# A two-stage spectral and feed-forward kernel: first group closed on chip by selection matmuls, weights and a third of the next input read early, other reads held

## The chip, the cores and the metric

The kernel runs on one core of a Trainium2 chip. The metric is the device time of one execution in microseconds. The profile of a run covers one execution, and its span is some 1.9 us shorter than the device time of the same run.

Some words. PE is TensorE, the engine of the matmuls; PSUM is the memory that it writes to, and an eviction is the copy of a result out of it. A clock of 1.00 is TensorE's full clock. The DMA share is the mean busy share of the 16 DMA engines, with each packet counted whole where it starts, so that it can pass 1.

## The reference

For each of 8 batches of 3136 tokens by 256 channels: a global filter in the frequency domain along the tokens, then a low-rank mixing along the tokens and a feed-forward along the channels.

```python
X = np.fft.rfft(x, axis=1)
Y = X * (filt_r + 1j * filt_i)[None, :, :]
y = np.fft.irfft(Y, n=3136, axis=1)          # per batch: 3136 x 256
...
h = y.transpose(0, 2, 1) @ U @ V             # rank 32 along the tokens
u = y + h.transpose(0, 2, 1)
out = u + np.maximum(u @ w_ch1, 0.0) @ w_ch2 # 256 -> 1024 -> 256
```

## The kernel before

The transform of length 3136 is split as 64 x 49. Stage 1 (64-point) writes its result to memory (ct1), stage 2 (49-point) reads it back in another order (tile a), its product with the filter goes through stage 3 to memory again (ct2), and stage 4 reads that (tile e) and makes the transposed input `ut` of a feed-forward group of 512 tokens. So every batch but the first makes two trips through memory before its first group. Batch 0 turns its stage 1 result on the chip and makes one.

The main loop is written by hand in steps. A group has 8 steps; each makes one 128-row tile of the first layer (two matmuls, ended by one ReLU on ScalarE) and a part of the second layer of the group before. All other work is hung onto steps:

```python
for n, gr in enumerate(groups):
    for t in range(8):
        for f, a in early[8 * n + t]: f(*a)     # products with the filter
        mm1(gr, t)                              # first layer, one tile, ReLU on ScalarE
        if n + 1 < len(groups) and t in ((2, 6) if n != 5 else (6, 7)):
            stage4(groups[n + 1], ...)          # input of the next group
        if n: mm2_part(groups[n - 1], t)        # second layer of the last group
        for f, a in plan[8 * n + t]: f(*a)      # stages 1 to 3 and reads of later batches
```

PE takes its instructions in this order and none can pass another. If the data of one small matmul are not there, the whole feed-forward stops. What is hung where, in before (cut):

```python
if b == 2: plan_st1(b, 12, (0, 1, 3, 4, 5, 7))               # stage 1 of batch 2 from step 12
elif b > 2: plan_st1(b, later(start[b - 1], -60))
m = later(start[b - 1], (5, -9, -12)[min(b, 3) - 1])         # stage 2 of batch b
...
# in stage 1 of batch b: the reads of x of batch b + 1
if 1 < b < NB - 1 and c: load_x(b + 1, c - 1)
```

Batch 1 starts at step 48 and batch 2 at step 104. I date step n by the start of its ReLU in the trace.

## Time and profile before

| | before |
|---|---|
| device time | 552.9 to 557.4 us, median 555.2 of 3 |
| first ReLU (step 0) | 62.6 us |
| step 8 (second layer joins) | 72.5 us |
| step 48 (batch 1) | 135.8 us |
| step 104 (batch 2) | 201.1 us |
| end of the span | 555.2 us |

The prediction shows the lines of the first 135 us. Here are, from the same view of windows, the two stretches after it: batch 1, then batches 2 to 7. Columns as there.

```profile
135.00:200.40 65.40, 63.91 (x567) 46.92 (x566) 43.07 (x48) 49.23 (x94) 36.11 (x22) 1.00 0.70 179
200.40:555.20 354.80, 347.32 (x3118) 259.43 (x3116) 222.91 (x256) 249.81 (x457) 159.13 (x89) 1.00 0.56 157
```

In the stretch of batch 1 PE lacks 1.5 us of being always busy.

### The profile page before, as it was taken

What the parts mean: (1) busy time and instruction counts of PE and PEld (TensorE: products, weight loads), DVE (VectorE), ACT (ScalarE), POOL (GpSimd) and SP (SyncE); (2) the same over time, 40 slices, a digit from 0 to 9 for tenths busy, and PEclk for the clock granted to TensorE, in tenths of its full rate; (3) what the DMA queues carried; (4) which work ended last, traced back from release to release, by engine and by line L of the source; (5) the groups of instructions that cost most, each with busy time, mean ns of one, the idle gap of its engine ahead of it and who ended that gap; (6) DMA issues with size and microseconds to landing.
All of it is one profiled execution on the core that took longest, in us unless ns stands there. A gap on an engine that the chain in (4) does not pass through costs nothing.

```text
span 555.2 us, 11638 instructions
## 1 busy us (share of the span) xinstructions
PE 517.2 (93%) x4491; PEld 375.3 (68%) x4491; DVE 353.1 (64%) x409; ACT 390.8 (70%) x684; POOL 282.4 (51%) x194
## 2 busy tenths in 40 slices
PE   5976689997999999999999999999999999999996
PEld 2634356664767777777776777777786777777775
DVE  6764675755756686758846785858746887643332
ACT  8566868774777688767776788677777577765663
POOL 5778179951883165915683175806563297300000
PEclk9999899997999999999999999999999999999999
DMA  9998876894669468774879468865653553333212
GB/s 194 157 170 192 225 141 187 209 230 130 174 184 250 125 176 199 173 204 137 193 222 221 123 173 228 166 199 152 186 170 121 141 167 121 106 113 115 96 77 87
DMA packets 85432, 92.06 MB, mean 166 GB/s; under 512 B 6741, under 2 KB 69416, under 8 KB 85376
## 3 DMA queue, kind: packets, MB, share of 16 engines
q1 hardware_dynamic: 67968, 75.12, 45.5%
q0 software_dynamic: 16960, 15.91, 19.1%
q8 instruction: 35, 0.57, 0.4%
q10 hardware_dynamic: 448, 0.28, 0.3%
q14 instruction: 21, 0.17, 0.1%
HBM read 57.42 MB, written 49.77 MB: 193 GB/s over the span
## 4 chain that ended last, share of the span: by engine, by line
PE 70%; POOL 10%; DVE 7%; DMA 6%; ACT 4%; issue 2%; DVEq 0%; ACTq 0%; POOLq 0%; SPq 0%
PE psum L521 25%; PE psum L488 24%; PE psum L352 4%; PE psum L344 4%; PE psum L477 4%; PE psum L497 3%; PE psum L266 3%; POOL y L634 3%; DMA x<-in_x_dram 3%; POOL x L170 2%; DVE ut L482 1%; DVE tb L632 1%; PE psum L416 1%; DMA w1sb<-in_moe_w_ch_dram 1%; ACT asb L273 1%
## 5 line engine op out<-in xcount | busy, mean ns | idle before, releaser
L492 ACT ACTIVATE hring<-psum 128x512 f16<-128x512 f32 (+1 forms) x416 | 237.7, 576 | 104.5 <-PE psum L488 103.2
L488 PE MATMUL psum<-ut,w1sb 128*128 128x512 f16 (+1 forms) x832 | 240.3, 370 | 6.4 <-ACT hring L492 3.0
L521 PE MATMUL psum<-w2sb,hring 128*128 128x256 f16 x1536 | 230.9, 273 | 0.0
L634 POOL TENSOR_TENSOR y<-ta,tb 128x1024 f16<-128x1024 f16 x56 | 120.5, 2159 | 159.4 <-DVE tb L632 115.5
L521 PEld LDWEIGHTS <-hring 128*128 128x128 f16 x1536 | 143.3, 98 | 63.8 <-issue 3.8
L482 DVE CAST ut<-psum 128x512 f16<-128x512 f32 x96 | 71.1, 741 | 108.3 <-PE psum L477 88.2
L488 PEld LDWEIGHTS <-w1sb 128*128 128x128 f16 x832 | 104.6, 145 | 27.3 <-issue 10.4
L529 DVE COPY och<-psum 128x512 f32<-128x512 f32 x96 | 66.2, 689 | 47.3 <-PE psum L497 46.6
L326 ACT CAST esb<-psum 98x512 f16<-98x512 f32 x128 | 74.7, 586 | 21.6 <-PE psum L344 16.0
L628 DVE TENSOR_TENSOR ta<-psum,fb 128x1024 f16<-128x1024 f32 x41 | 50.0, 1218 | 7.9 <-PE psum L352 6.9
L273 ACT CAST asb<-psum 128x512 f16<-128x512 f32 x78 | 45.7, 589 | 12.3 <-PE psum L266 11.2
L497 PE MATMUL psum<-idn,ut 128*128 128x128 f16 x392 | 54.0, 220 | 0.0
L477 PEld LDWEIGHTS <-e 96*128 96x128 f16 x768 | 35.9, 99 | 25.5 <-issue 10.2
L630 DVE TENSOR_TENSOR tb<-psum,fc 64x1024 f16<-64x1024 f32 x41 | 50.3, 1226 | 0.9
L632 DVE TENSOR_TENSOR tb<-psum,fc 64x1024 f16<-64x1024 f32 x41 | 49.9, 1218 | 0.8
L477 PE MATMUL psum<-sv,e 96*128 96x64 f16 x768 | 38.8, 194 | 6.5 <-DMA e<-ct 3.7
L344 PE MATMUL psum<-y,g 128*98 128x512 f16 x105 | 39.9, 380 | 3.0 <-POOL y L634 1.5
L497 PEld LDWEIGHTS <-ut 128*128 128x128 f16 x392 | 38.4, 98 | 4.9
L628 POOL TENSOR_TENSOR ta<-pc,fb 128x1024 f16<-128x1024 f16 x15 | 32.4, 2159 | 10.7 <-ACT pc L638 10.7
L352 PE MATMUL psum<-a,w2t 98*128 98x512 f16 x113 | 34.3, 379 | 1.7 <-DVE tb L632 1.6
L266 PE MATMUL psum<-x,wf 128*128 128x256 f16 x168 | 31.3, 274 | 2.8 <-DVE asb L271 1.0
L630 POOL TENSOR_TENSOR tb<-pc,fc 64x1024 f16<-64x1024 f16 x15 | 31.8, 2122 | 1.2
(93 smaller groups left out, 373.6 us busy)
## 6 DMA issues: line engine op xcount, KB each, us to landing
out_dram<-och SPq DMA_DIRECT2D x47, 512.0 KB
ct<-esb SPq DMA_DIRECT2D x64, 196.0 KB
x<-in_x_dram POOLq DMA_DIRECT2D x48, 256.0 KB, 8.1
e<-ct SPq DMA_DIRECT2D x48, 256.0 KB
a<-ct SPq DMA_DIRECT2D x56, 196.0 KB
ct<-asb SPq DMA_DIRECT2D x42, 256.0 KB
wf<-wf SPq DMA_DIRECT2D x3, 256.0 KB
w1sb<-in_moe_w_ch_dram POOLq DMA_DIRECT2D x1, 512.0 KB, 6.8
```

Of the source, the lines that this page charges most:

```text
L326: nc.scalar.copy(esb[b, k][:, 2 * half:2 * half + 2, :].rearrange("p s d -> p (s d)"), pe[0:98])
L344: nc.tensor.matmul(pe[0:98], g3[:, m, :], v, start=(n == 0), stop=(n == len(parts) - 1))
L477: nc.tensor.matmul(pu[:, 64 * i:64 * i + 64], e2[b, c][:, i, 128 * dh:128 * dh + 128], sv[:, 64 * r:64 * r + 64], start=(i == 0), stop=Tru ...
L482: nc.vector.tensor_copy(o, v)
L488: nc.tensor.matmul(ph[:, 0:n], w1sb[:, dh, :, t], gr.ut[:, dh, 0:n], start=(dh == 0), stop=(dh == 1))
L492: nc.scalar.activation(h[:, 0:n], ph[:, 0:n], RELU)
L497: nc.tensor.matmul(o[:, dh * 128:dh * 128 + 128], gr.ut[:, dh, t0:t0 + n], idn, start=False, stop=(dh == 1), skip_group_check=True)
L521: nc.tensor.matmul(o, gr.h[tt][:, i * 128:(i + 1) * 128], w2sb[:, tt, :], start=(tt == 0), stop=False, skip_group_check=True)
L529: nc.vector.tensor_copy(gr.och[:, 2 * y:2 * y + 2, :].rearrange("p j d -> p (j d)"), gr.pc)
L628: eng.tensor_mul(ta, p, va)
L630: eng.tensor_mul(tb[0:64], p[64:128], vb[64:128])
L634: nc.gpsimd.tensor_add(ys[k], ta, tb)
```

## The change

The intent is to start the feed-forward earlier. The core of the diff, with cuts marked:

```diff
+        def pick(j):                      # rows 48 to 63 of the first tile, from results on chip
+            for i in range(2):
+                sl = 2 * (j - 12) + i
+                for g in range(4):
+                    nc.tensor.matmul(zp[32 * g:32 * g + 32], sel[:, g, 28 - 4 * sl:60 - 4 * sl],
+                                     esb[0, j // 2][:, 2 * (j % 2) + i, :], start=(sl == 0), ...)
...
+                if k == 5:
+                    load_e2(0, 0, 48)     # only 48 of 64 rows go through memory
...
+    nc.gpsimd.dma_start(w2sb, moe_w_ch2...)   # second weight right behind the first
+        load_x(1, 0)                          # a third of x of batch 1 during stage 2 of batch 0
...
+    load_x(1, 1, e2[0, 0][0:1, 0, 0:1])       # the rest held until the first e tile is there
+    load_x(1, 3)
+    load_x(1, 2)
...
+    for n in (0, 3, 3, 4, 5, 5, 6, 7, 8, 9):
+        at(n, step1, 1)                       # most of stage 1 of batch 1 inside the groups
+    at(13, lambda: load_x(2, 0, a2q[0][0:1, 0:1]))
...
+    at(50, lambda: load_x(3, 0, groups[6].h[0][0:1, 0:1]))   # x of batch 3 held for batch 1's first ReLU
+    for c in range(1, 4):
+        at((50, 52, 54)[c - 1], load_x, 3, c)
...
-            plan_st1(b, 12, (0, 1, 3, 4, 5, 7))
+            plan_st1(b, 18, (0, 3, 4, 5, 7))
-            plan_st1(b, later(start[b - 1], -60))
+            plan_st1(b, later(start[b - 1], -46 if b == 3 else -60), ...)   # batch 3: from step 52
-        m = later(start[b - 1], (5, -9, -12)[min(b, 3) - 1])
+        m = later(start[b - 1], (16, -2, -12)[min(b, 3) - 1])
...
-            if n + 1 < len(groups) and t in ((2, 6) if n != 5 else (6, 7)):
+            turns = {0: (5, 6), 5: (6, 7), 12: (6, 7)}.get(n, (2, 6))
```

Cut are: the compact stage 1 table, widened on chip; the filter copies in quarters, some on GpSimd; the products on 113 partitions; the doubled form of stages 2 and 3 for four of the eight parts of batch 1.

## The prediction

> **What bounds the kernel now.** I read the windows first, cut at the landmarks of the program: the first product of batch 0's stage 2 (25.1 us), the last stage 3 of batch 0 (48.7), the first matmul of the feed-forward groups (61.2), the first product of the second layer (72.0), the first group of batch 1 (134.9), the end. Columns: stretch, its us, busy us (instructions) of each engine, TensorE clock, DMA share.
>
> ```profile
> core 0: us, PE busy (x) PEld busy (x) DVE busy (x) ACT busy (x) POOL busy (x), PEclk, DMA share, GB/s
> 0.00:25.10 25.10, 17.93 (x136) 11.68 (x137) 16.78 (x26) 16.81 (x12) 15.82 (x30) 1.00 1.02 179
> 25.10:48.70 23.60, 18.60 (x102) 9.88 (x102) 14.29 (x13) 15.90 (x24) 18.39 (x21) 0.93 1.04 178
> 48.70:61.20 12.50, 8.41 (x80) 4.99 (x80) 5.69 (x8) 8.44 (x12) 5.69 (x1) 0.86 0.81 217
> 61.20:72.00 10.80, 5.70 (x42) 3.15 (x39) 9.75 (x18) 7.78 (x10) 4.97 (x8) 1.00 0.88 198
> 72.00:134.90 62.90, 55.21 (x462) 39.30 (x462) 40.47 (x45) 42.72 (x77) 42.32 (x25) 0.95 0.75 177
> 134.90:555.20 420.30, 411.33 (x3683) 306.35 (x3681) 266.08 (x303) 299.12 (x550) 195.23 (x111) 1.00 0.58 160
> ```
>
> The last row is the bound: from 134.9 us PE is busy 411 of 420 us at full clock, and some 4 us of the rest is the tail. Nothing the change does can shorten that part. All that can be won lies before 134.9: 61.2 us until the first feed-forward matmul, 10.8 us in a group without a second layer, 62.9 us for the other five groups of batch 0.
>
> The timeline tells what paces the first part.
>
> ```profile
> 28.94 0.73 POOL L226 DMA_DIRECT2D w1sb<-in_moe_w_ch_dram  x1
> 36.00 0.57 POOL L384 DMA_DIRECT2D w2sb<-in_moe_w_ch_dram  x1 [2.07 <-DMA w1sb<-in_moe_w_ch_dram]
> 36.59 4.21 POOL L397 TENSOR_TENSOR uv<-pc,fb 128x1024 f16<-128x1024 f16 x2
> 38.77 0.59 PE L344 MATMUL psum<-uv,g 128*98 128x512 f16 x2 [2.46 <-POOL uv L397]
> 41.00 1.06 PE L344 MATMUL psum<-uv,g 128*98 128x512 f16 x2
> ...
> 52.45 1.10 SPq L438 DMA_DIRECT2D e<-ct  x2
> 57.03 2.72 PE L234 MATMUL psum<-wf 128*128 128x512 f16 x6 [0.45 <-ACT al L285]
> 61.22 0.41 PE L488 MATMUL psum<-ut,w1sb 128*128 128x512 f16 x1
> ```
>
> GpSimd could not issue the load of the second weight until the first had landed (35.7), so its product of stage 2 came late, PE idled 2.46 us, and the pair of matmuls that takes 0.59 us then took 1.06. After the last stage 3 the result goes to memory and back (e is asked for at 52.45), while PE does stage 1 of batch 1 and dummy matmuls, until 61.2. The DMA share of about 1 says that a shorter instruction chain alone would not bring this forward: the loads must shrink or be reordered.
>
> The chain of waits shows the end of batch 0.
>
> ```profile
> 102.76 2.12 POOL tb L630
> 104.94 2.13 POOL tb L632
> 107.14 1.95 POOL y L634
> 109.21 1.52 POOL x L170 x3
> 111.10 0.64 POOL x L170
> 111.74 0.54 POOL xl L163
> 112.28 2.16 POOL y L634
> 119.76 6.48 DMA ct<-esb
> 126.38 3.58 DMA e<-ct
> ```
>
> GpSimd's products and the issuing of x of batch 3 (109.2 to 112.3) delay stage 3 of batch 1. Its last store takes 6.5 us beside those 1.6 MB, and the first group of batch 1 waits 3.7 us for its data.
>
> **What the skill says.** "TensorE: Matmul & The Clock Gate", section on the HAM clock gate: PE falls to half rate after an idle window of about 3.4 us and needs one busy window to recover. The trace agrees in kind: 0.93 and 0.86 around the pause at 36.3, though that was only 2.46 us. "VectorE: DVE Perf Modes", "Why PSUM operands drop a tier": a product reading f32 PSUM runs at one element per cycle. The trace agrees: 1.22 us for 1024 elements, so fewer partitions (113 for 128) save nothing. "DMA: Bandwidth & Descriptors", "Anatomy of one DMA": about 2 us fixed per transfer, mostly the receipt. The e read's 3.58 us for 256 KB at a busy time fits, so a memory round trip cannot be below some 5 us; the change takes it off the path.
>
> **The change part by part.**
>
> *Loads.* The queue table gives 19.1% of 555 us for 15.91 MB on the GpSimd queue (6.7 us per MB of f16 landed, the f32 source being twice that) and 45.5% for 75.12 MB on the SP queue (3.4 us per MB). Check on before: wf 2.8, small constants 0.9, sv and kr 1.4, U 1.3, x 10.5, filters 10.5, V 1.3, w1 3.5, two stores 1.3: 33.5, plus a 2 us start, 35.5; w1 landed at 35.7. After: wf compact (0.41 MB) 1.4, U as f32 1.35, constants with the selection tables 1.5, x 10.5, filters 10.5, V 1.3, w1 3.5, one store 0.7: w1 at 32.5. Then w2 3.5 and the last filter row 0.5: 37. Then a third of x of batch 1, 3.5: 41.5. The other two thirds (7 us of engine time) are held until the first tile of batch 0 has come back.
>
> *Stage 2 of batch 0.* Only two transposed tiles, not four, precede the first product, and x lands 2 us sooner; VectorE must first finish a quarter of the U work (3 instructions, 1.5 us). First product at about 22.7, for 25.1. VectorE now takes 15 of 16 products (15 x 1.22) and one copy (0.7): 19 us, so the last ends at 41.9, for 47.4 by GpSimd. The last filter row (37) is in time for it. GpSimd's one product waits for its 7 us copy of V, started once w1 has landed: 39.6 + 2.1, just in time.
>
> *Closing of group 0.* Rows 48 to 63 of the first tile come from the four result tiles on chip: 64 small selection matmuls (the 32 of the low rank took 1.06 us: about 2 us), one 0.37 us copy, two 512-column matmuls. Only 48 rows pass through memory, from stores finished earlier: store 6 at about 39.5, landed 43, read back by 45.5. Then 16 matmuls 0.8, tables 0.43, a stage 1 step 0.2, low rank 0.43, eviction 0.75. First feed-forward matmul at about 48.5, for 61.2: gain 12.7.
>
> *Group 0.* Before, PE waited for 8 filter copies of 0.7 us on VectorE and four of 1.9 on ScalarE. They now lie in quarters on GpSimd and in later gaps. But ten stage 1 steps of batch 1 move in here (2 PE matmuls of 0.11 and one 0.6 or 0.7 copy each), and x must arrive: 45.5 + issue 1 + 3.5 + other traffic, 51 to 52 for the second third and 56 for the last. Eight evictions of 0.6 would be 5 us; I take 9.5, with 3 us of waits. Gain 1.3 of 10.8.
>
> *Groups 1 to 5.* PE work by counts: 40 steps x (0.43 + 0.44 + 0.055) 37; stage 4, 5 x 0.8, 4; stage 1 of batches 1 and 2, 3.3; low rank 1.1; stages 2 and 3 of batch 1, of which four of eight parts now use the doubled form (four matmuls of 0.216 more in each part, 0.86), 10.4 in all, 3.5 more than before. Sum 55.8 us. Waits I add: 2 us where stage 2 first needs batch 1 (its last stage 1 store stands on the GpSimd queue behind eight filter copies), 1 to 2 us at the first group of batch 1. x of batch 3 is held past that group, and the last parts use no GpSimd product, so the store there should take 3 us, not 6.5. 59.5 us, for 62.9: gain 3.4.
>
> *After.* The schedule starts stage 2 of batch 2 seven steps later, and five stage 1 steps of batch 3 move behind the landmark: 2 us lost.
>
> Sum: 12.7 + 1.3 + 3.4 - 2 = 15.4; 555.2 - 15.4 = 539.8, rounded to 539 for the clock (0.86 and 0.95 in two stretches cost some 4 us, of which I expect back a little).
>
> **The rivals.** (1) The wait moves to x of batch 1. Withholding two thirds until 45.5 makes stage 1 late; PE takes its instructions in order, so group 0 would stall at its fourth and seventh step. For it: the DMA share near 1 up to 72. Against: the steps are spread for these arrivals. It would cost 3 to 6 us more, 543 to 546. (2) The start is DMA-bound and gains little: if selection tables, stores and reads queue behind the weights, group 0 starts at 53. For it: the byte sum leaves only some 2 us of slack at 45. 544. (3) GpSimd becomes the bound in groups 1 to 5: filter copies at the rate of its V copy (6.95 us for 3136 elements) would take 2.2 us each, 18 us in all, delaying the last store of stage 1 and thus stage 2. Three to five us, 543. (4) All waits close: the 55.8 us stand, group 0 takes 7.5, start at 47.5: 532.
>
> **Range and chances.** The 2% line is 544.1. The start is surest (two thirds of its gain follow from removed work), the waits least. Rivals 1 to 3 together pass the line, one alone hardly. I say 539, range 531 to 548; faster 0.75, same 0.22, slower 0.03.
>
> **What would show it.** First product of stage 2 at 22 to 23.5 us, VectorE without gaps to 42; first feed-forward matmul at 47.5 to 50 with the clock near 1; w2 landed before 39; group 0 in 8 to 11 us with waits on x; first group of batch 1 at 116 to 121; from there 420 to 423 us. Wrong would be: a start after 53, a wait of over 4 us on x or on a (rivals 1, 3), or a last part longer by over 4 us, which would mean that lateness was passed on to batches 2 and 3.

## The result, and the profile after

The changed kernel took 560.9 to 562.8 us, median 561.6 of 4 runs, against a median of 555.6 of 4 for before. The ratio is 1.011, 95% interval 1.007 to 1.016. Ratios are the mean time of one kernel's fast runs over that of the other's of the same rounds, so not quite the ratio of the medians. The change is 1.1% slower; I had said 3% faster.

The windows of the changed kernel, cut at the same landmarks: first product of stage 2, last stage 3 of batch 0, first feed-forward matmul, first product of the second layer, batch 1, batch 2, end.

```profile
0.00:22.50 22.50, 13.07 (x123) 8.08 (x124) 16.51 (x26) 10.50 (x14) 15.31 (x29) 1.00 1.01 175
22.50:43.50 21.00, 20.09 (x152) 10.53 (x150) 17.63 (x16) 14.51 (x22) 15.30 (x13) 1.00 0.94 176
43.50:48.20 4.70, 4.70 (x56) 2.48 (x55) 2.63 (x5) 2.23 (x4) 2.68 (x6) 1.00 0.76 176
48.20:58.60 10.40, 6.57 (x48) 3.86 (x46) 5.20 (x10) 5.17 (x10) 9.35 (x10) 1.00 1.11 220
58.60:125.00 66.40, 58.55 (x478) 40.53 (x477) 40.26 (x55) 41.40 (x75) 32.11 (x27) 0.97 0.72 178
125.00:205.00 80.00, 67.52 (x575) 48.23 (x575) 48.03 (x52) 51.65 (x98) 49.34 (x34) 0.96 0.75 177
205.00:560.30 355.30, 347.83 (x3119) 259.40 (x3117) 221.99 (x254) 250.09 (x457) 159.05 (x89) 1.00 0.57 155
```

Read it from the top. The start is what it was meant to be: 48 us to the feed-forward, for 61, with PE busy nearly all the time from 22.5 us on and the clock at 1.00 where before had 0.93 and 0.86. The last row is the old one, within half a microsecond. The loss is in the row of batch 1: 80.0 us, for 65.4, with 12.5 us of PE idle for 1.5, and the clock at 0.96. The row above it is 3 us longer than its counterpart too. In sum, by the ReLU dates:

| stretch | before | after | difference |
|---|---|---|---|
| to step 0 | 62.6 | 48.5 | -14.1 |
| steps 0 to 8 | 9.9 | 10.6 | +0.8 |
| steps 8 to 48 | 63.4 | 66.6 | +3.2 |
| steps 48 to 56 | 10.3 | 18.2 | +8.0 |
| steps 56 to 104 | 55.0 | 61.8 | +6.8 |
| step 104 to the end | 354.1 | 354.6 | +0.4 |

What PE waited for between 125 and 206 us in the changed kernel (total us, times, longest):

```profile
PE psum L305 <- DMA x<-in_x_dram: 5.9, 1, 5.9
PE psum L599 <- DVE ut L604: 1.6, 1, 1.6
PE psum L305 <- DVE ut L604: 1.5, 1, 1.5
PE psum L610 <- DVE ut L604: 1.1, 1, 1.1
PE psum L400 <- DVE tb L741: 1.0, 1, 1.0
```

Before, no wait in that stretch was listed with more than 0.5 us in total. L305 is stage 1, and x is the input of batch 3. The timeline shows how that wait comes about and what follows it:

```profile
128.41 2.13 POOL L743 TENSOR_TENSOR y<-ta,tb 113x1024 f16<-113x1024 f16 x1 [15.71 <-DVE tb L741]
...
129.88 1.13 ACT L614 ACTIVATE hring<-psum 128x512 f16<-128x512 f32 x2
...
130.49 0.18 POOL L185 COPY x<-hring 1x1 f16<-1x1 f16 x1
...
130.97 2.52 POOL L187 DMA_DIRECT2D x<-in_x_dram  x4 [0.30 <-POOL x L185]
...
136.68 0.58 PE L305 MATMUL psum<-x,wf 128*128 128x256 f16 x2 [5.93 <-DMA x<-in_x_dram]
137.06 1.06 PE L610 MATMUL psum<-ut,w1sb 128*128 128x512 f16 x2
...
139.41 0.94 PE L610 MATMUL psum<-ut,w1sb 128*128 128x512 f16 x2
```

The read stands at step 50 of the plan and is issued at 131.0. The first matmul that needs it stands at step 52, and the read's second half landed at 136.5, 4.9 us after its issue. PE stands still until 136.7, and the feed-forward pair that takes 0.59 us takes 1.06 and 0.94 for three more microseconds.

Part of the delay is made in GpSimd's queue. The read is held for the first ReLU of batch 1 (step 48), which ended at 126.3. GpSimd took its instructions in order, and in front of the read stood an addition of stage 2 of batch 2 (the first line above), whose inputs VectorE had ready only at 128.3. It ended at 130.5, and then came the one-element copy that is the hold. So 4.2 us passed between the end of that ReLU and this copy. An estimate from these times: with the read issued 4.2 us earlier and as long on its way, the wait would have been some 1.8 us in place of 5.9. No run moved the read in front of that addition, so this stays untested.

And in the stretch before, after step 15:

```profile
71.44 0.67 PE L400 MATMUL psum<-a,w2t 98*128 98x512 f16 x2 [4.28 <-DMA a<-ct]
...
71.91 1.06 PE L610 MATMUL psum<-ut,w1sb 128*128 128x512 f16 x2
```

The same pattern: the first product of stage 2 of batch 1 waits 4.3 us for tile a, and the clock falls behind it.

### The profile page after: what moved, and what is told of

Same layout as the page of the kernel before. It is cut to its first block, busy times and chain, and to the rows that moved or that the text cites. A ratio compares the mean times of both kernels' runs of the same rounds, so it can differ in the third digit from the quotient of the medians.

```text
span 560.3 us, 11729 instructions
## 1 busy us (share of the span) xinstructions
PE 518.3 (93%) x4540; PEld 373.1 (67%) x4540; DVE 352.2 (63%) x413; ACT 375.5 (67%) x678; POOL 283.1 (51%) x206
## 4 chain that ended last, share of the span: by engine, by line
PE 55%; POOL 5%; DVE 1%; ACT 1%; issue 1%; DMA 1%; ACTq 0%; POOLq 0%
PE psum L643 21%; PE psum L610 20%; PE psum L619 3%; PE psum L599 3%; PE psum L400 3%; PE psum L392 2%; PE psum L305 2%; POOL y L743 1%; POOL x L187 1%; PE psum L537 1%; POOL ta L737 1%; POOL tb L741 1%; POOL tb L739 1%; DMA a<-ct 1%; DVE tb L741 0%
## 5 line engine op out<-in xcount | busy, mean ns | idle before, releaser
L743 POOL TENSOR_TENSOR y<-ta,tb 113x1024 f16<-113x1024 f16 x52 | 112.3, 2164 | 154.9 <-DVE tb L741 118.4
L604 DVE CAST ut<-psum 128x512 f16<-128x512 f32 x94 | 69.7, 741 | 105.4 <-PE psum L599 88.3
L599 PEld LDWEIGHTS <-e 96*128 96x128 f16 x752 | 34.5, 97 | 24.5 <-issue 9.2
L737 DVE TENSOR_TENSOR ta<-psum,fb 113x1024 f16<-113x1024 f32 x37 | 45.1, 1218 | 8.3 <-PE psum L400 7.0
L739 DVE TENSOR_TENSOR tb<-psum,fc 49x1024 f16<-49x1024 f32 x37 | 45.4, 1226 | 1.0
L741 DVE TENSOR_TENSOR tb<-psum,fc 49x1024 f16<-49x1024 f32 x37 | 45.1, 1218 | 1.0
L400 PE MATMUL psum<-a,w2t 98*128 98x512 f16 x120 | 36.8, 383 | 7.4 <-DMA a<-ct 4.3
L599 PE MATMUL psum<-sv,e 96*128 96x64 f16 x752 | 37.3, 192 | 5.8 <-DVE ut L604 1.6
L305 PE MATMUL psum<-x,wf 128*128 128x256 f16 x168 | 32.2, 275 | 9.9 <-DMA x<-in_x_dram 8.0
L392 PE MATMUL psum<-y,g 113*98 113x512 f16 x98 | 37.4, 381 | 2.8 <-POOL y L743 1.6
L737 POOL TENSOR_TENSOR ta<-pc,fb 113x1024 f16<-113x1024 f16 x15 | 32.4, 2161 | 14.1 <-ACT pc L747 14.0
L187 POOL DMA_DIRECT2D x<-in_x_dram x48 | 30.7, 655 | 5.3 <-DMA w1sb<-in_moe_w_ch_dram 3.1
```

The lines of the kernel that those rows point to most:

```text
L400: nc.tensor.matmul(pz, w, a, start=True, stop=True)
L599: nc.tensor.matmul(pu[:, 64 * i:64 * i + 64], e2[b, c][:, i, 128 * dh:128 * dh + 128], sv[:, 64 * r:64 * r + 64], start=(i == 0), stop=Tru ...
L604: (nc.scalar.copy if gr is groups[0] and dh else nc.vector.tensor_copy)(o, v)
L737: eng.tensor_mul(ta, p[0:NZ], va)
L739: eng.tensor_mul(tb[0:NR], p[64:NZ], vb[64:NZ])
L743: nc.gpsimd.tensor_add(ys[k], ta, tb)
```

## The experiments

Seen so far are two large waits on reads. A wait that is seen need not be time that can be had back. The main theory, A: the loss is the read of x of batch 3, put too close to its use. Rivals: B, PE would have met another lateness (stage 2 of batch 2, planned seven steps later than before); C, the hold of x of batch 1 does the harm; D, it is DMA time that is short between batch 1 and batch 3; E, the early start is worth little, because the DMA engines set when later data come; F, distances in the schedule are too short. All results below are correct but one, which is told.

### Run 1: x of batch 3 ten steps earlier

```diff
-    at(50, lambda: load_x(3, 0, groups[6].h[0][0:1, 0:1]))
-    for c in range(1, 4):
-        at((50, 52, 54)[c - 1], load_x, 3, c)
+    for c in range(4):
+        at((40, 41, 42, 43)[c], load_x, 3, c)
```

> The changed kernel with x of batch 3 asked for at steps 40 to 43, ungated, in place of steps 50 to 54 behind the first ReLU of batch 1. Theory A (the loss is the read of x of batch 3, too late for stage 1 of batch 3 at step 52): the 5.9 us PE wait there goes, with it some 3 us of half clock after it, so 551 to 554 us against 561.6; against that the round trip of batch 1 meets this read again and its wait may grow from 1.4 to 3 or 4 us. Rival B (the wait is only slack that PE would spend on stage 2 of batch 2, which starts 7 steps late, so the lateness comes out at the group before batch 2): under 3 us gained, 558 to 561.

Measured: 562.6 us, ratio 1.010 (1.006 to 1.013). No gain. The wait on x is gone, and between 110 and 140 us there is this instead:

```profile
PE psum L599 <- DMA e<-ct: 6.9, 1, 6.9
```

It was 1.4 us in the changed kernel. Asked for at step 40, the 1.6 MB of x travel beside the last store and the first reads of batch 1's way through memory. The hold at step 50 had a purpose: it protects that trip. My fear was of 3 to 4 us, and it was 6.9, all of the gain.

### Run 2: the read left, its use later

```diff
-            plan_st1(b, later(start[b - 1], -46 if b == 3 else -60), (0, 3, 4, 5, 7) ...)
+            plan_st1(b, later(start[b - 1], -41 if b == 3 else -60), (0, 1, 3, 4, 5, 7) ...)
```

> The changed kernel with the read of x of batch 3 where it is, but stage 1 of batch 3 started at step 57 instead of 52 and packed closer. Theory A: same gain as with the early read, without its collision: wait on x gone, 551 to 554 us. Rival B: 558 to 561. If the early read gains and this does not, the packing of stage 1 into fewer steps is what costs.

Measured: 560.8 us, ratio 1.008 (1.003 to 1.014). The step dates tell more than the total. Step 56 came at 135.5, for 144.0, and at step 80 it was still 6.9 us ahead. Then, from 170 us on, the waits were:

```profile
PE psum L400 <- DMA a<-ct: 2.5, 1, 2.5
PE psum L599 <- DVE ut L604: 1.6, 1, 1.6
PE psum L305 <- DVE ut L604: 1.5, 1, 1.5
```

The first is stage 2 of batch 3: stage 1 ended at step 81 and its result had not been through memory when it was wanted at step 92. By step 104 only 1.4 us were left of 8.5. So neither place that was tried for the use suits the read at step 50: at step 52 PE waits for x, at step 57 it waits for what is made of x. Neither run supports A as I first put it, that moving either end of the distance would do. (Both show that the wait on x costs time where it stands: without it, steps 48 to 56 took 10.9 and 9.5 us, for 18.2.)

### Run 3: stage 2 of batch 2 five steps earlier

```diff
-        m = later(start[b - 1], (16, -2, -12)[min(b, 3) - 1])
+        m = later(start[b - 1], (16, -7, -12)[min(b, 3) - 1])
-            at(later(s, (-7, -5, -5)[k] if b == 2 else -9), fetch, k)
+            at(later(s, (-3, -2, -2)[k] if b == 2 else -9), fetch, k)
```

> The changed kernel with stage 2 of batch 2 started 5 steps earlier (step 41 instead of 46), all else as it is, the wait on x of batch 3 included. Theory A alone: within 1.5 us of the changed kernel. Rival B (lateness of stage 2 of batch 2 is what costs at steps 80 to 104, where the changed kernel is 5 us slower than before): 556 to 559 us, with the stretch from step 80 to 104 shorter by 3 to 5 us and the wait on x of batch 3 unchanged at about 6 us.

Measured: 566.3 us, ratio 1.017 (1.014 to 1.021), slower than the changed kernel, which neither theory had. Its first reads of a now stand at steps 38 and 39, in front of the trip of batch 1, and the wait on e grew to 3.6 us, with 1.2 on a. That these reads delay e is my reading; no run separates the two. The wait on x was 7.4: GpSimd, with more of stage 2 in front of the read, issued it only 6.4 us after the end of the ReLU that it is held for. Steps 56 to 104 took 60.1 us for 61.8, so B holds for a small part only.

### Run 4: the hold of x of batch 1 undone

```diff
         load_x(1, 0)
+        load_x(1, 1)
+        load_x(1, 3)
+        load_x(1, 2)
...
-    load_x(1, 1, e2[0, 0][0:1, 0, 0:1])
-    load_x(1, 3)
-    load_x(1, 2)
```

> The changed kernel with the hold undone: all of x of batch 1 is asked for where its first third is. If holding pays, as I assumed: the first tile of batch 0 comes back 4 to 7 us later, first feed-forward matmul at 52 to 55 us in place of 48.2, though the wait for batch 1 at step 15 (4.3 us) shrinks to under 1; net 0 to 3 us slower, 561 to 565. Rival C (the hold only moves the wait to step 15): net gain of 2 to 4 us, 557 to 560.

Measured: 567.4 us, ratio 1.018 (1.014 to 1.023), slower by more than I had for the hold. Step 0 came at 53.3 for 48.5, but not because the first tile came back late: PE waited 5.1 us there for GpSimd's one product of batch 0. The added reads stand in front of the copy of V in GpSimd's queue, and that copy, which takes 7 us, began at 36.1 for 32.5. Group 0 took 7.3 us for 10.6, since its x was there, so step 8 was only 1.5 us later; 4 us more were lost after it. The wait on a at step 15 was still 4.1 us, for 4.3, where the expectation had it under 1. So rival C falls in the form that the hold moves a wait to step 15. Whether the hold pays by itself stays open: reads placed behind the copy of V were not tried.

### Run 5: x of batch 3 in the gap

Between 89 and 113 us the changed kernel's DMA share is 0.76, then 0.56. The read is put there in thirds, ahead of the trip of batch 1.

```diff
+    for c in range(4):
+        at((24, 28, 32, 33)[c], load_x, 3, c)
```

> The changed kernel with x of batch 3 asked for in thirds at steps 24, 28, 32 (and the last row at 33), where the DMA engines of the changed kernel have some four tenths free (84 to 112 us). The two runs before moved the wait: asked for at 40 it meets the round trip of batch 1 (wait on e 1.4 to 6.9 us), used later it makes stage 2 of batch 3 late. Theory D (it is one DMA queue time that is missing between batch 1 and batch 3, and the gap can hold it): wait on x at step 52 gone, wait on e under 3 us, 552 to 556 us. Rival B (the last stretch before batch 2 is bound by the late stage 2 of batch 2, whatever x does): step 104 stays at 203 to 206 us, 559 to 562.

Measured: 556.8 us, ratio 0.999 (0.992 to 1.006). The whole loss against before is gone. Its three stretches (group 0, groups 1 to 5, batch 1):

```profile
45.70:57.60 11.90, 7.30 (x50) 4.17 (x49) 6.96 (x11) 5.69 (x11) 9.74 (x11) 0.97 1.09 220
57.60:124.40 66.80, 60.59 (x478) 41.59 (x477) 39.85 (x54) 41.08 (x74) 36.40 (x34) 0.93 0.86 198
124.40:196.90 72.50, 66.06 (x578) 47.94 (x577) 47.73 (x51) 51.66 (x98) 44.88 (x26) 1.00 0.67 172
```

Batch 1 takes 72.5 us for 80.0, the clock is 1.00 for 0.96, there is no wait on x, and the wait on e was 2.1 us. The DMA share of the stretch before rose from 0.72 to 0.86: the gap was there to be used. So A holds in this form: the read must land before step 52 and must not travel with batch 1's data, and there was room for both; with that, D falls. The 7.5 us are the 5.9 us wait and what the clock lost after it: they lie between steps 48 and 56, which took 10.7 us for 18.2.

### Run 6: the gap, stage 2 of batch 2 five steps earlier, stage 4 at the usual steps

The edits of runs 5 and 3 together, and the entry `12: (6, 7)` taken out of `turns`.

> As the run before, and stage 2 of batch 2 five steps earlier, and stage 4 of the first group of batch 2 at the usual steps 2 and 6 again in place of 6 and 7. Theory D with B (both are needed): 546 to 551 us, step 104 at 190 to 195 us. If only x counts: as the run before. If the read of stage 2 meets the round trip of batch 1: wait on e or a over 4 us near step 46, and no gain.

Measured: 555.1 us, ratio 0.998 (0.989 to 1.007), far from my 546 to 551. Steps 48 to 104 took 68.3 us for 72.5, as hoped, but step 48 came at 131.6, with waits of 3.7 us on e and 2.4 on a near step 46. The last sentence of the expectation came true in substance: the two waits are 6.1 us in all, though neither is over 4 by itself.

### Run 7: a late start on purpose

```diff
-    keep_warm(3, psum[:, 7, :])
+    keep_warm(40, psum[:, 7, :])
```

> The changed kernel with 37 more dummy matmuls (8.0 us of PE at 0.216 each) just before its first feed-forward matmul, the loads issued as before. If PE sets the end from there on, as my prediction had it: 8 us later, 569 to 570 us. Theory E (the early start is worth little, because x of batch 1 and stage 2 of batch 1 come at a time that the DMA engines set): the two waits on x, the one on sv and the one on a at step 15, 7.8 us together, take the delay up: 0 to 3 us later, 561 to 565.

Measured: 567.7 us, ratio 1.020 (1.013 to 1.026); in the trace the end came 5.8 us later. Neither number was right: step 0 came 7.4 us later, group 0 took up 3.3 of it (its x and sv were there), and from step 8 to step 56 the delay grew again from 4.0 to 5.8 us. What matters is the wait on a, in the window from 75 to 110 us:

```profile
PE psum L400 <- DMA a<-ct: 4.7, 1, 4.7
```

It is as long as with the early start, and so was the wait on x of batch 3, 6.0 us. Had the DMA engines set the time of these data, a delay of 8 us would have swallowed the waits. They move along with the steps, so they are distances between steps that are too short for the way between them. For x this had to be so, since its read is held for the ReLU of step 48; the wait on a is the test. E falls for all but group 0: of 8 us of start, 5.8 reach the end, and the losses are not the price of starting early.

### Run 8: run 5, and the two halves of one stage 4 apart

Near step 102 stand two waits on ut, 1.6 and 1.5 us. There the changed kernel has both halves of stage 4 of batch 2's first group at steps 6 and 7, on one PSUM bank.

```diff
-            turns = {0: (5, 6), 5: (6, 7), 12: (6, 7)}.get(n, (2, 6))
+            turns = {0: (5, 6), 5: (6, 7), 12: (3, 6)}.get(n, (2, 6))
```

> As the run with x of batch 3 in the gap, and only stage 4 of the first group of batch 2 moved from steps 6 and 7 to steps 3 and 6 of the group before. If the two waits on the eviction of that stage 4 (1.6 and 1.5 us near step 102) come from its two halves standing side by side on one PSUM bank: 2 to 3 us less than that run, step 96 to 104 in 11 to 12 us for 14.1. If they come from the late stage 2: a wait on e or on the low-rank rows of e takes their place and nothing is won.

Measured: 555.0 us, ratio 0.994 (0.986 to 1.002). Its row of batch 1:

```profile
128.50:199.20 70.70, 65.81 (x578) 47.88 (x577) 46.73 (x51) 51.66 (x98) 44.88 (x26) 1.00 0.67 170
```

1.8 us less than run 5, with steps 96 to 104 in 12.2 us for 14.1. The halves side by side were the cause, as the first sentence had it. (In the profiled execution step 48 was 4 us later than in run 5: 1.7 of it from the start, 1.3 from group 0, 1.1 from the stretch after. The two kernels are alike up to there, so this is what single executions differ by.)

### Run 9: and stage 2 of batch 2 two steps earlier

As run 8, with `(16, -4, -12)` and the three first reads left at steps 39, 41 and 41.

> As the run before, and stage 2 of batch 2 two steps earlier, its first three reads where they are. Steps 56 to 104 then in 57 to 59 us for 61.8 (the kernel before: 55.0), the wait on e of batch 1 at 2 us as in the gap run; 549 to 553 us. If the read of the fourth part, now at step 44, meets the round trip: wait on e over 3.5 us and no gain over the run before.

Measured: 553.7 us, ratio 0.993 (0.987 to 1.000). Steps 48 to 104 took 70.7 us, the same as run 8. The wait on e was 1.4 us. My 57 to 59 us for steps 56 to 104 were wrong: 60.3.

### Runs 10 to 12: the wait on a taken away

Stage 2 of batch 1 starts at step 18 in place of 15, stage 1 of batch 2 at 23, x of batch 3 at 25 to 35, with the stage 4 of run 8 and stage 2 of batch 2 at its step 46.

```diff
-            for k, q, d in ((3, 17, 26), (5, 21, 31), (2, 23, 33), (4, 28, 37)):
+            for k, q, d in ((3, 20, 28), (5, 24, 34), (2, 26, 36), (4, 30, 38)):
-            for k, qs in ((0, (15, 16)), (1, (19, 20)), (6, (33, 34)), (7, (36, 37))):
+            for k, qs in ((0, (18, 19)), (1, (22, 23)), (6, (34, 35)), (7, (36, 37))):
-            plan_st1(b, 18, (0, 3, 4, 5, 7))
+            plan_st1(b, 23, (0, 1, 3, 4, 5, 7))
```

> The gap and the stage 4 of the runs before, and stage 2 of batch 1 begun at step 18 instead of 15, so that nine steps and not six lie between its last stage 1 step and its first product, with stage 1 of batch 2 at step 23 on, and the sign copies of the filters off VectorE's way at steps 5 to 11. Theory F (the wait on a is a distance in the schedule, stage 1 to stage 2, shorter than the way through memory of about 10 us, since 8 us of delay left it at 4.7): the wait on a goes to under 1 us, step 48 at 118 to 121 us, 545 to 550 us in all. If the data come at an absolute time that the DMA engines set: the wait only moves to another read, step 48 at 124 to 126.

Run 10 gave a wrong result: I had put four sign copies of the filter after the copies that overwrite their source. The instructions and their sizes are as they should be, so its time can be read: 551.1 us, ratio 0.988 (0.982 to 0.994). The wait on a was gone, so F holds. But step 48 came at 124.4, not at 118 to 121.

Run 11 has the copies in the right order, and 5 of 12 evictions of stage 1 of batch 2 on VectorE.

> The late start of stage 2 of batch 1 again, with the sign copies ahead of the copies that overwrite their source (the run before had four of them after, and its result was wrong though its time stands), and 5 of the 12 full evictions of stage 1 of batch 2 on VectorE in place of ScalarE. In that run the wait on a was gone (4.3 to 0) but ScalarE's evictions came late at steps 20 to 40 (waits of 2.3 and 2.0 us) and step 48 stood at 124.4. If ScalarE was full there: step 48 at 119 to 122, 546 to 549 us. If PE's own work fills those steps: 550 to 552 as before it.

Measured: 554.2 us, ratio 0.993 (0.987 to 0.998), step 48 at 125.9. The waits on ScalarE's evictions became waits on VectorE's. Run 12 is run 11 with all those evictions back on ScalarE.

> The late start of stage 2 of batch 1 with the sign copies put right and all full evictions of stage 1 of batch 2 on ScalarE again, as in the first such run. If its ratio of 0.988 was the schedule and not the chip: 0.985 to 0.991, the best of all, and correct. If the last run's 0.993 is what this schedule gives whichever engine evicts: 0.990 to 0.996, and step 48 at 124 to 126 once more, so that taking away the wait on a has only let the next limits show.

Measured: 553.0 us, ratio 0.993 (0.989 to 0.997), step 48 at 125.1. The second half of the expectation holds. Its waits from 75 to 112 us:

```profile
PE psum L599 <- ACT asb L309: 2.3, 4, 1.3
PE psum L392 <- ACT esb L370: 2.0, 3, 0.7
PE psum L400 <- DVE uv L766: 1.0, 3, 0.4
```

The wait on a of 4.3 us has been traded for small waits on evictions, presumably since the same stage 1, 2 and 3 work now stands in fewer steps. In six of the thirteen kernels, step 48 came between 124.4 and 126.0, whether or not they had that wait. Whether another arrangement of steps 15 to 48 would pass that, these runs don't settle.

The dates of the steps in the kernels that carry the argument, each from its one profiled execution:

| kernel | step 0 | 8 | 48 | 56 | 104 | end |
|---|---|---|---|---|---|---|
| before | 62.6 | 72.5 | 135.8 | 146.1 | 201.1 | 555.2 |
| changed | 48.5 | 59.2 | 125.7 | 144.0 | 205.8 | 560.3 |
| run 1, x early | 47.5 | 59.0 | 131.8 | 142.7 | 204.7 | 560.3 |
| run 2, use late | 47.1 | 60.0 | 126.0 | 135.5 | 204.4 | 558.9 |
| run 5, x in the gap | 46.3 | 58.2 | 125.0 | 135.7 | 197.5 | 552.0 |
| run 7, late start | 55.9 | 63.2 | 130.9 | 149.8 | 211.6 | 566.1 |
| run 8, stage 4 apart | 48.0 | 61.2 | 129.1 | 139.9 | 199.8 | 554.3 |
| run 12, a later | 47.6 | 60.3 | 125.1 | 135.9 | 195.8 | 550.3 |

Runs 9, 11 and 12 beat both kernels, by 0.7% against before and 1.8% against the changed one (1.0114 over 0.993), by ratios taken in different rounds. Against before their intervals end just under 1, that of run 9 at 0.9995.

## Why the prediction was wrong, point by point

**The start: right.** First product of stage 2 at 22.1 us (I had 22.7), the last one on VectorE ended at 41.4 (41.9), first feed-forward matmul at 47.85 (48.5). The second weight landed at 34 us (37): the byte sums per queue were good to some 3 us. The rival of a DMA-bound start fell. One sum had a slip: 37 and 3.5 us make 40.5 and not 41.5 for the first third of x, which landed at 39.7.

**Group 0: nearly right.** 11.1 us from its first matmul to the first product of the second layer, where I had 9.5. The waits were on x, 2.0 us, as named, and on sv, 1.5 us, the stage 4 table whose larger part the change reads after the last results, and which I had left out.

**Groups 1 to 5: the size was off.** 59.5 predicted, 66.3 measured from second layer to batch 1. I added 2 us for the first product of stage 2; the wait was 4.3 us and matmuls at half clock behind it. In its row PE was idle 7.9 us, for 3.7 in my sum, and busy 58.6, for 55.8. My reason was wrong too. I blamed eight filter copies on GpSimd, perhaps 2.2 us each; they took 1.03 us and were done at 57 us. The last store was issued at 63.8, after a VectorE eviction, and the way from there to tile a (7.6 us) is longer than the steps left for it. Run 12 shows that the wait can be removed and that what it covered then shows itself. Rival 3 named the right place, with the wrong engine, and its sign, a wait of over 4 us on a, came.

**The step that failed is the one headed "After".** It says that stage 2 of batch 2 starts seven steps later and that five stage 1 steps move behind the landmark: "2 us lost". Measured: 435.1 us from 125.2 to the end, for 420.3, so 14.8. I priced moved matmuls and asked of no moved read whether it lands in time. The line that held x of batch 3 I had even counted as a gain for batch 1 ("held past that group"), without looking at what waits for that x: stage 1 of batch 3 at step 52, two steps behind it. Nor did I look at what stands in front of that read in GpSimd's queue: the addition of stage 2 of batch 2, behind which the freed read stood for 4.2 us. By the rows of batch 1:

- 7.5 us: the wait on x of batch 3 and the clock after it. Taken away by run 5 (80.0 to 72.5).
- 1.8 us: stage 4 with its halves side by side. Taken away by run 8 (72.5 to 70.7).
- 5.4 us are left over before (70.7 to 65.3). The idle time of PE is 4.9 us there and 1.5 in before, so 3.4 of it; the other 2 are PE busy for longer, with some 10 more matmuls in the row. An earlier stage 2 of batch 2 took some of it away (run 6: 68.3) and gave it back as waits before step 48. Which of the small waits could go without that, stays open.

The rest is half a microsecond after step 104.

**The rivals and the margin.** I wrote that a last part longer by over 4 us would show lateness passed on to batches 2 and 3. That is where it was, but "passed on" is not what happened: run 7 delayed the start by 8 us and found the waits on a and on x as long as before. They are set by the plan of the steps, not by the early start. I had no rival for a read that the change itself moves, and the range, whose top was 548, came from waits before batch 1 only.

**The facts of the chip that it rested on.** They held in the main; they were used in too few places. The products from PSUM took 1.22 us on 113 partitions, as expected. The clock did stay at 1.00 through the start; I had not asked where else PE would stop, and after the 5.9 us wait the pairs ran at 1.06 and 0.94 us until about 140. One reading of the clock was wrong: the 0.86 of the stretch from 48.7 does not belong to the pause at 36.3. After that pause the clock was at half from 40.0 to 43.4 us; the 0.86 is a second fall, from 57.0 to 60.4. The times of transfers I had added up for the start, and not for the read that the change puts two steps before its use.

## What to carry to other kernels

In a hand-made in-order schedule, price every read that a change moves by the distance from its issue to its first user, in microseconds of steps, by what stands in front of it in the queue that issues it, and by what else travels in that time; a saved stretch upstream says nothing on it. A wait that is seen is not yet time to be had: here one read had three places, and two of them only moved the wait. To learn whether a wait comes from the data's arrival or from the schedule, delay the start by a known amount: if the wait stays as long, it is the schedule.

## What the Trainium skill lacked or had wrong

- "TensorE: Matmul & The Clock Gate" gives, in its part on the HAM clock gate, an idle window of about 3.4 us before the clock falls. In the kernel before, a pause of 2.46 us was enough: the clock was at half from 40.0 to 43.4 us, with pairs at 1.06 us for 0.59. From 57.0 to 60.4 us it was at half again, after 3.4 us in which PE was busy for 1.7 us and no pause was longer than 1.0. The page says that the window runs freely, which may be why; as a budget for a pause, 3.4 us is too generous here.
- "DMA: Bandwidth & Descriptors" prices one transfer alone in its section on the anatomy of one DMA, and has no number for a store and a read that depends on it while other reads are under way. Here the wait at the end of such a trip was 1.4 us without and 6.9 us with a 1.6 MB read beside it (run 1).
